# One side-work list for a whole sliding layer, stepped layer norm, and quads loaded across the chunk border, in a four-layer attention kernel

## The chip, the cores and the metric

The kernel runs on one core of a Trainium2 chip. The metric is the device time of one execution in microseconds (us). Before the change the median of three runs is 2695.69 us (2692.45 to 2696.52).

The engines are named as the profile names them: PE is the tensor engine (PEld its weight loads), DVE the vector engine, ACT the scalar engine, POOL the general engine, SP the engine that issues all the kernel's DMAs, in order (SPq is its queue).

## The reference

Four attention layers follow one another on one sequence of 2048 rows of 512: sliding, full, sliding, full. The two kinds have their own weights, each used twice. All have 32 heads of 16.

```python
def layer(x, wqkv, wo, sliding):
    h = (x - mean(x)) / sqrt(var(x) + 1e-5)              # layer norm without weights
    q, k, v = (h @ wqkv).reshape(S, 3, 32, 16)           # per head
    s = q @ k.T * 16 ** -0.5
    if sliding:                                          # 0 <= i - j < 256
        s = where(mask, s, -1e9)
    return x + (softmax(s) @ v).reshape(S, 512) @ wo

x = layer(layer(layer(layer(x, A, sliding), B, full), A, sliding), B, full)
```

## The kernel before

The sequence is cut into four **chunks** of 512 queries, and the heads into eight **quads** of four. A sliding layer runs `for c in chunks: for qd in quads: three steps`. One **step** (`attn_win`, L826) computes scores for two pairs of heads on PE (`exps`, L755, the matmuls of L768), takes the exponential on ACT (L772), lets POOL clear the edges of the window (L840, L843), and two steps later multiplies by V on PE (L850). After a quad, `epilogue` (L718) normalises the result on DVE.

Everything else is **side work** that fills PE between the steps: projections K and Q (`project`, L491), V (`values`, L640), and the output product with the residual sum (`wo`, L677). Its operands are split into two half-precision parts, so one projection is 48 groups of four matmuls (L406, 128 x 32 by 512 columns each). `mms` gives them out in pieces of four groups, 16 matmuls. K and Q go through memory: they are written there by SP (L539 to L543) and read again by quad in the order attention wants them (`load_win`, L794: three transfers, q, k and the k of the window's older half). After a K or Q, its squares are summed on PE (L559), and DVE reduces them to bounds (L575, L593, L601); that closing part waits in a list, `pend`, and `settle` (L606) issues it. `wo` is followed by layer norm of the same rows for the next layer: statistics (L439), scales, then four **parts** (`norm`, L442: L455 twice, L461) on DVE, and then four transposing DMAs on SP (`transposed`, L479, work `T`). Layer 0's own norms are the works `NN`.

The order of PE's instructions is written out by a planner when the kernel is built. It keeps a model clock (`clock`, advanced by `spent`), and each piece of side work is a generator (`Work`, L858) with a planned cost, dependencies, and the time at which it is ready. `K`, `Q`, `V` and the output product have a weight tile of 1 MB each, in a ring of two buffers; `may_open` (L884) says when a work may start loading it. A work that is `aside` is advanced by one item at each step, whatever the budget. `Side` (L919) holds the list: at each `step` it spends pieces until `cost * k / (steps - 2)` is reached, taking the first work in the list that is ready. `finish` (L1005) runs whatever is left, without attention between. The other engines' order is made by the framework's scheduler from the program order, priorities and its own model of times.

Before the change, each chunk of a sliding layer has a `Side` of its own with a list of its own (`side0(c)`, `side2(c)`, L1191 and L1200), finished when the chunk ends; only then are the first two quads of the next chunk loaded (L1042 to L1044). Within a chunk, quads are loaded two ahead, into rings of three.

Of the kernel before, what the change touches and what calls it, by code (L numbers as in the profile page):

```python
# [19 lines left out]
P = 128  # L20
NT = S // P
NC = D // P
HT = P // DH
NHT = H // HT
# [166 lines left out]
def fast_path(ctx, tc, flag, a_x, a_wqkv, a_wo, b_wqkv, b_wo, out):  # L191
# [250 lines left out]
    def norm(l, c, xs, tail=False):  # L442

        mv, y, nb, out = ST[l, c][1], [], [], []

        def scales():
            y.append(rsqrt(nc, vp, f"{l}_{c}", mv[:, :, 1]))
            if tail:
                nb.append(vp.tile([P, 4], F32, name=f"nb{l}_{c}", tag="lnb", bufs=1))
                nc.vector.scalar_tensor_tensor(nb[0], mv[:, :, 0], -1.0, y[0], op0=ALU.mult, op1=ALU.mult)  # L450

        def parts(i):
            xn = vp.tile([P, D], F32, name=f"xn{l}_{c}_{i}", tag="xn", bufs=1)
# [7 lines left out]
            nc.vector.tensor_tensor(xh[:, 1], xn, xh[:, 0], ALU.subtract)  # L461
            if tail:
                transposed(l, c, i, xh)
            else:
                out.append(xh)
        yield from turns(2, (2.4, scales), *[(1.8, lambda i=i: parts(i)) for i in range(4)])
        XN[l, c] = out
        XNR[l, c] = clock[0] + (0 if (l, c) == (0, 1) else 2 if PH["full"] else 9)
# [97 lines left out]
    def keys(l, c, act, ht=None, then=None, ring=0):  # L566
        sqs = yield from project(l, 1, c, act, ht, ring)

        def rest():
            ph = squares(f"k{l}_{c}_{ht}", sqs)  # L570
            if l not in KM:
                KM[l] = vp.tile([P, NQ], F32, name=f"km{l}", tag="km", bufs=2)
            r = quarters(ht)
            with tc.high_priority(HEAD_START):
                nc.vector.tensor_reduce(KM[l][r, c:c + 1], ph[r], axis=AX.XY if PH["full"] else AX.X, op=ALU.max)  # L575
                if then is not None:
                    then(l, ht)
        pend.append((clock[0] + (4.6 if PH["full"] else 3.6 if PH["win"] else 1.2), rest))

    def queries(l, c, act, ht=None, ring=0):  # L580
        sqs = yield from project(l, 0, c, act, ht, ring)

        def rest():
# [20 lines left out]
        pend.append((clock[0] + (4.6 if PH["full"] else 3.6 if PH["win"] else 1.2), rest))  # L604

    def settle(all_=True):  # L606
        while pend and (all_ or pend[0][0] <= clock[0]):
# [250 lines left out]
    class Work:  # L858
# [24 lines left out]

        def may_open(self):  # L884

            return (all(d in DONE for d in self.deps if d[0] == "P") and
                    all(d[1:] in ONR or d[1] % 2 == 0 and d[2] for d in self.deps if d[0] == "O") and
                    all(("N",) + d[1:] in DONE for d in self.deps if d[0] == "T") and
                    (len(wused[self.ring]) < RINGS[self.ring] or wused[self.ring][-RINGS[self.ring]].done or wused[self.ring][-RINGS[self.ring]].freed) and not (PH["win"] and self.ring)
                    and not (self.adds and any(x.adds and not x.done for x in wused[0])))  # L890
# [6 lines left out]
        def advance(self):  # L897
# [127 lines left out]
    def attention(l, works):  # L1025
# [91 lines left out]
    def OO(l, c, tail=False):  # L1117
        return Work(later(wo, l, c, tail), PO, ("N", l + 1, c), [("O", l, c, NHT - 1), ("P", l % 2, 3)], True)

    def NN(c, after=()):  # L1120
        def gen():
# [69 lines left out]
    def side0(c):  # L1191
        if c == 0:
            return [F((kw[1], True), (qs[0, 1], False), (kw[2], True), (qs[0, 2], False)), K(0, 1), Q(0, 1), PR(0, 3, [("K", 0, 1)]), VV(0, 1), PR(1, 1, [("V", 0, 1, (0, 1), 0)]), NN(2, [("T", 0, 1)]), T(0, 2)]
        if c == 1:
            return [F((kw[3], True), (qs[0, 3], False)), K(0, 2), NN(3), T(0, 3), OO(0, 0), Q(0, 2), PR(1, 0, [("P", 0, 3)]), VV(0, 2), PR(1, 2, [("P", 1, 1)]), T(1, 0), PR(1, 3, [("P", 1, 0)])]
        if c == 2:
            return [F(*[(kf, True, k, k + 1) for k in range(NQ)]), K(0, 3), OO(0, 1), Q(0, 3), VV(0, 3), K(1, 0), T(1, 1)]
        return [F(*[(qs[1, k], False) for k in range(NQ)]), K(1, 1), OO(0, 2), VV(1, 0, True, (0,)), T(1, 2), K(1, 2), Q(1, 0)]
# [26 lines left out]
    def side3(t, c):  # L1225
# [8 lines left out]
        if (t, c) != (0, 0):  # L1234
            a.append(O3(c - 1, t) if c else O3(3, t - 1))
        return a

    works = [[side0(c) for c in range(NQ)], [[last_lower(1), K1(2), upper(1, 2), upper(1, 3), K1(3)], side1()], [side2(c) for c in range(NQ)],
             [side3(t, c) for t in range(NHT) for c in range(NQ)]]
    late = lambda l: [("N", l, 3)]  # L1240
    tails = {0: [VV(1, 2, True, (0,)), OO(0, 3, True), VV(1, 1, True, (0, 1), late(1)), VV(1, 0, True, (1,), late(1)), T(1, 3), K1(0, True), K1(1, True)],
# [55 lines left out]
```

## Time and profile before

| what | us |
|---|---|
| median of three runs | 2695.69 |
| the profiled execution's own time | 2692.26 |
| its span, first to last instruction | 2690.2 |
| PE busy in the span | 2474.9 |
| ACT busy | 2363.6 |
| DVE busy | 1107.5 |
| POOL busy | 531.8 |
| first sliding layer, first to last exponential | 50.2 to 405.1 |
| second sliding layer, first to last exponential | 1406.7 to 1462.9 for its first chunk, to 1662.6 for its last |

The mean granted PE clock is 0.991 over the span. How to read the rows shown below: a row of the 40 slices gives the busy share in tenths of 1/40 of the span each. A row of busy time by stretches begins with the stretch, from and to in us, and its length; then come the busy us of PE, PEld, DVE, ACT and POOL with instruction counts in brackets (of PE alone where only PE was asked for), the granted PE clock as a share of full speed, the busy share of the DMA engines and GB/s. A row of waits names engine, operation and line, after the arrow what it waited for, then the total in us, how often, and the longest. A row of a timeline gives start, length, engine, line, operation, written and read tiles, shape and count; instructions of a kind that follow one another are merged.

### The profile page before, as it was taken

What the parts mean: (1) busy time and instruction counts of PE and PEld (TensorE: products, weight loads), DVE (VectorE), ACT (ScalarE), POOL (GpSimd) and SP (SyncE); (2) the same over time, 40 slices, a digit from 0 to 9 for tenths busy, and PEclk for the clock granted to TensorE, in tenths of its full rate; (3) what the DMA queues carried; (4) which work ended last, traced back from release to release, by engine and by line L of the source; (5) the groups of instructions that cost most, each with busy time, mean ns of one, the idle gap of its engine ahead of it and who ended that gap; (6) DMA issues with size and microseconds to landing.
All of it is one profiled execution on the core that took longest, in us unless ns stands there. A gap on an engine that the chain in (4) does not pass through costs nothing.

```text
span 2690.2 us, 120844 instructions
## 1 busy us (share of the span) xinstructions
PE 2474.9 (92%) x54767; PEld 1133.5 (42%) x54767; DVE 1107.5 (41%) x2350; ACT 2363.6 (88%) x2671; POOL 531.8 (20%) x1072
## 2 busy tenths in 40 slices
PE   7889999999998999999999999899999999999997
PEld 3344444444443444444444444544444443433332
DVE  5576453223334434434236666232333323333333
ACT  4666764999999999999996776699999999999997
POOL 1556550000000100100116886010000000000000
PEclk9999999999999999999999999999999999999999
DMA  8889875232334325324227666433333323334332
GB/s 281 254 274 268 236 198 155 69 97 86 110 94 120 97 91 148 103 87 115 92 77 211 189 171 166 128 95 105 98 97 97 106 77 114 106 98 126 126 118 93
DMA packets 341189, 361.29 MB, mean 134 GB/s; under 512 B 117800, under 2 KB 256568, under 8 KB 334392
## 3 DMA queue, kind: packets, MB, share of 16 engines
q1 hardware_dynamic: 340664, 353.46, 44.2%
q8 instruction: 430, 7.05, 1.1%
q14 instruction: 95, 0.78, 0.1%
HBM read 240.65 MB, written 96.99 MB: 126 GB/s over the span
## 4 chain that ended last, share of the span: by engine, by line
ACT 55%; PE 23%; issue 11%; DVE 6%; DMA 3%; SPq 1%; POOL 0%; ACTq 0%; DVEq 0%; POOLq 0%
ACT e L772 55%; PE b L406 7%; PE acc L850 4%; PE acc L817 3%; PE s L764 2%; PE s L768 2%; PE bs L409 2%; PE b L409 2%; PE b L402 1%; DMA kt<-kw 1%; DVE xh L461 1%; DVE xn L455 0%; DMA qs<-sp 0%; SPq L483 0%; DVE xh L455 0%
## 5 line engine op out<-in xcount | busy, mean ns | idle before, releaser
L772 ACT ACTIVATE e<-s 128x1024 f32<-128x1024 f32 (+2 forms) x2432 | 2241.6, 1056 | 143.2 <-PE s L768 104.5
L817 PE MATMUL acc<-e,vt 64*17 64x512 f32 x16384 | 1094.6, 590 | 1.9 <-issue 1.9
L764 PE MATMUL s<-qt,kt 64*32 64x512 f16 x16384 | 860.0, 381 | 123.9 <-ACT e L772 97.1
L764 PEld LDWEIGHTS <-kt 64*32 64x32 f16 x16384 | 408.2, 89 | 935.1 <-issue 853.8
L817 PEld LDWEIGHTS acc<-e,vt 64*17 64x17 f32 x16384 | 283.8, 92 | 67.9 <-issue 8.1
L843 POOL TENSOR_SCALAR_AFFINE_SELECT e<-e 128x256 f32<-128x256 f32 x512 | 230.5, 457 | 154.8 <-ACT e L772 154.1
L840 POOL TENSOR_SCALAR_AFFINE_SELECT e<-e 128x256 f32<-128x256 f32 x448 | 201.5, 456 | 96.5 <-ACT e L772 93.2
L850 PE MATMUL acc<-e,vt 128*17 128x384 f32 (+2 forms) x2816 | 202.6, 390 | 2.5 <-POOL e L840 2.2
L749 POOL TENSOR_TENSOR oh<-o,oh 128x512 f16<-128x512 f32 x31 | 36.1, 1165 | 725.1 <-DVE oh L748 725.1
L428 DVE TENSOR_SCALAR sa<-acc 128x512 f32<-128x512 f32 x64 | 44.3, 691 | 291.3 <-PE acc L817 291.3
L406 PE MATMUL b<-xc,w 128*32 128x512 f16 x2496 | 152.4, 389 | 10.8 <-DVE km L575 6.9
L714 DVE SCALAR_TENSOR_TENSOR x<-b,x 128x512 f32<-128x512 f32 x122 | 84.0, 689 | 175.1 <-PE b L402 168.4
L534 POOL TENSOR_TENSOR sq_h<-sp_h 128x512 bf16<-128x512 f16 x29 | 43.0, 1483 | 562.4 <-DVE sp_h L528 562.4
L768 PE MATMUL s<-qt,kt 64*128 64x384 f16 (+2 forms) x1408 | 120.8, 276 | 28.2 <-ACT e L772 22.7
L534 POOL TENSOR_TENSOR sq<-sp 128x512 bf16<-128x512 f16 x32 | 45.8, 1434 | 496.8 <-DVE sp L528 473.6
L402 PE MATMUL b<-xc,w 64*32 64x512 f16 x3072 | 126.4, 376 | 1.5 <-DVE j L429 0.8
L428 DVE TENSOR_SCALAR vt<-b 128x256 f32<-128x256 f32 (+1 forms) x36 | 18.4, 512 | 233.8 <-PE b L402 219.9
L402 PE MATMUL b<-wo,oh 64*32 64x512 f16 x2592 | 109.1, 376 | 4.1 <-DVE m_None L591 1.8
L402 PE MATMUL b<-xc,w_h 64*32 64x512 f16 x2784 | 111.8, 376 | 0.1
L428 DVE TENSOR_SCALAR j_h<-b 128x512 f32<-128x512 f32 x29 | 20.1, 692 | 214.6 <-PE b L402 214.6
L406 PEld LDWEIGHTS <-w 128*32 128x32 f16 x2496 | 73.5, 99 | 79.2 <-issue 27.7
L768 PEld LDWEIGHTS <-kt 64*128 64x128 f16 x1408 | 52.2, 94 | 125.7 <-issue 105.3
(142 smaller groups left out, 1942.3 us busy)
## 6 DMA issues: line engine op xcount, KB each, us to landing
kt<-kf SPq DMA_DIRECT2D x128, 512.0 KB
qt<-qs SPq DMA_DIRECT2D x128, 256.0 KB
xd<-x SPq DMA_DIRECT2D x96, 256.0 KB
x<-xd SPq DMA_DIRECT2D x96, 256.0 KB
w<-wd SPq DMA_DIRECT2D x21, 1024.0 KB
kt<-kw SPq DMA_DIRECT2D x64, 256.0 KB
qs<-sp SPq DMA_DIRECT2D x48, 256.0 KB
wo<-wd SPq DMA_DIRECT2D x12, 1024.0 KB
```

The source lines that it names most:

```text
L402: nc.tensor.matmul(ps[g:g + 32, r], a[k, g:g + 32], b[k], start=(i == 0), stop=(i == len(pairs) - 1), skip_group_check=True)
L406: nc.tensor.matmul(ps[g:g + 32], a[:, g:g + 32], b, start=(i == 0), stop=(i == len(pairs) - 1), skip_group_check=True)
L409: nc.tensor.matmul(ps, a, b, start=(i == 0), stop=(i == len(pairs) - 1))
L534: nc.gpsimd.tensor_tensor(sq, sp[:, 0], sp[:, 0], ALU.mult)
L714: nc.vector.scalar_tensor_tensor(xs[i], p, 1 / WS, xs[i], op0=ALU.mult, op1=ALU.add)
L764: nc.tensor.matmul(ps[g:g + 32, h], kt[R * h:R * h + R, pr, kc + g:kc + g + 32], qt[R * h:R * h + R, pr], start=True, stop=True, skip_grou ...
L768: nc.tensor.matmul(ps[:, h, s0:s0 + wd_], kt[R * h:R * h + R, pr, kc:kc + P], qt[R * h:R * h + R, pr, qc:qc + wd_], start=True, stop=True)
L772: nc.scalar.activation(e[:, :, w0:w1], ps[:, :, w0:w1], AF.Exp, scale=SCALE)
L817: nc.tensor.matmul(acc[r][32 * h:32 * h + DH + 1, :], V[l, qd // 4, j // 8][k, j % 8, 4 * (qd % 4) + h, :], es_[h // 2][k, h % 2, :], star ...
L840: nc.gpsimd.affine_select(v, v, pattern=[[0, 2], [-1, P]], compare_op=ALU.is_gt, fill=0.0, base=0, channel_multiplier=1)
L843: nc.gpsimd.affine_select(v, v, pattern=[[0, 2], [1, P]], compare_op=ALU.is_ge, fill=0.0, base=0, channel_multiplier=-1)
L850: nc.tensor.matmul(a[32 * h:32 * h + DH + 1, q * P:(q + nb) * P], V[l, (4 * c + j) // 4][:, j % 4, 4 * qd + h, :], es_[h // 2][:, h % 2, s ...
```

## The change

There are four edits, for the sliding layers (0 and 2) only.

1. **One list.** `attention` makes one `Side` for all 96 steps of a sliding layer. Its works are listed for the layer; `finish` runs after the last chunk. In place of the finish at each chunk's end, a chunk begins when its own K, Q and first V are done (`needs`, `lacks`) and nothing of it is in `pend` (`owes`); else side work is forced until they are. Works that only move data or prepare weights are held until their chunk begins by a dependency on `("A", l, c, 0)`, which is set when a quad starts. Output products stand earlier in the lists, and may load their weights and rows from the sixth quad of the chunk on which they depend (for the product of layer 1's last chunk, from that layer's last quad).
2. **Next chunk's first quads.** During the last two quads of a chunk, the first two of the next are loaded, if that chunk lacks and owes nothing.
3. **Layer norm in steps.** In a sliding layer `norm` yields after the scales (2.6 us of model clock) and after each part (2.4), issues the transposes itself, each two parts behind, and leaves nothing to the work `T`. Before, the parts were 2.5 us apart and `T` began 9 us after the last, one transpose every 2.3 us.
4. **At every unit.** Once an output product has given its weight buffer back (`freed`), it becomes `aside`, so that its norm advances at every step.

```diff
         yield from turns(...)   # in norm(), ahead of this line:
+        if PH["win"] and not tail:
+            scales()
+            yield wait(2.6)
+            for i in range(4):
+                parts(i)
+                yield wait(2.4)
+                if i > 1:
+                    transposed(l, c, i - 2, out[i - 2])
+            yield wait(2.0)
+            transposed(l, c, 2, out[2])
+            yield wait(2.4)
+            transposed(l, c, 3, out[3])
+            XN[l, c], XNR[l, c] = (), clock[0]
+            return
...
-            return (all(d in DONE for d in self.deps if d[0] == "P") and
-                    all(d[1:] in ONR or d[1] % 2 == 0 and d[2] for d in self.deps if d[0] == "O") and
+            return (all(d in DONE for d in self.deps if d[0] in "PA") and
+                    all(d[1:] in ONR or (d[1] % 2 == 0 and ("A", d[1], d[2], NQD - 3) in DONE or ("A", 1, d[2], NQD - 1) in DONE and d[1:3] == (1, 3)) for d in self.deps if d[0] == "O") and
...
-                self.freed = self.freed or c[0] == "freed"
+                if c[0] == "freed":
+                    self.freed = self.aside = True
...
-        sd = None
+        sd, early = None, deque()
+        if win:
+            for c in range(1, NQ):
+                for w in works[c]:
+                    if w.aside and (w.name is None or w.name[0] == "P"):
+                        w.deps = [*w.deps, ("A", l, c, 0)]
+            sd = Side(3 * NQD * NQ, [w for c in range(NQ) for w in works[c]], works[NQ])
+        needs = lambda c: [("K", l, c), ("Q", l, c), ("V", l, c, (0, 1), 0)] if l or c else []
+        lacks = lambda c: any(n not in DONE for n in needs(c))
+        owes = lambda c: any(e[2] == (l, c) for e in pend)
...
                 else:
-                    sd = Side((3 if win else NT) * len(qds), works[t * NQ + c], works[t * NQ + c + 1], 0.34 if l == 3 and t < 2 else 0.0)
-                ahead = deque([PRE.pop("w", None) or load(l, c, qds[0])])
-                if win:
+                    while lacks(c):
+                        sd.one(True)
+                    if owes(c):
+                        settle()
+                ahead, early = early, deque()
+                if not ahead:
+                    ahead.append(PRE.pop("w", None) or load(l, c, qds[0]))
+                if win and len(ahead) == 1:
                     ahead.append(load(l, c, 1))
...
                     ops = ahead.popleft()
+                    DONE["A", l, c, qd] = clock[0]
                     if qd + 1 + win in qds:
                         ahead.append(load(l, c, qd + 1 + win))
+                    elif win and c + 1 < NQ and len(early) == qd - NQD + 2 and not lacks(c + 1) and not owes(c + 1):
+                        early.append(load(l, c + 1, len(early)))
...
-                if l != 1 or c == NQ - 1:
+                if l == 3 or c == NQ - 1:
                     sd.finish(l == 3 and (t, c) != (NHT - 1, NQ - 1))
...
         if c == 1:
-            return [..., K(0, 2), NN(3), T(0, 3), OO(0, 0), Q(0, 2), ...]
+            return [..., K(0, 2), NN(3, [("T", 0, 2)]), T(0, 3), OO(0, 0, after=[("T", 0, 3)]), Q(0, 2), ...]
         if c == 2:
-            return [F(...), K(0, 3), OO(0, 1), Q(0, 3), VV(0, 3), K(1, 0), T(1, 1)]
-        return [F(...), K(1, 1), OO(0, 2), VV(1, 0, True, (0,)), T(1, 2), K(1, 2), Q(1, 0)]
-    def side2(c):
-        if c == 0:
-            return [OO(1, 3), Q(2, 2), T(2, 3), K(2, 3)]
-        if c == 1:
-            return [OO(2, 0), Q(2, 3), T(3, 0), K3(0, 0, True)]
-        if c == 2:
-            return [OO(2, 1), VV(2, 3), T(3, 1), K3(1, 0, True)]
-        return [OO(2, 2), T(3, 2), Q3(0, 0, True), K3(2, 0, True)]
+            return [F(...), OO(0, 1), K(0, 3), Q(0, 3), VV(0, 3, after=[("A", 0, 2, 1)]), K(1, 0), T(1, 1)]
+        return [F(...), OO(0, 2), K(1, 1), VV(1, 0, True, (0,)), T(1, 2), K(1, 2), Q(1, 0)]
+    def side2():
+        return [OO(1, 3), OO(2, 0), OO(2, 1), OO(2, 2), Q(2, 2), T(2, 3), K(2, 3), Q(2, 3), VV(2, 3, after=[("A", 2, 2, 1)]),
+                T(3, 0), K3(0, 0, True), T(3, 1), K3(1, 0, True), T(3, 2), Q3(0, 0, True), K3(2, 0, True)]
```

In these lists `K(l, c)`, `Q`, `VV` and `OO` are the projections and the output product of layer `l` and chunk `c`, `K3` and `Q3` a quarter of one, `T` the transposes, `NN` layer 0's norm, `PR` weight preparation and `F` constant rows in memory.

More of the change, by code (lines that the diff above doesn't have):

```diff
@@ L577, in rest @@
                     then(l, ht)
-        pend.append((clock[0] + (4.6 if PH["full"] else 3.6 if PH["win"] else 1.2), rest))
+        pend.append((clock[0] + (4.6 if PH["full"] else 3.6 if PH["win"] else 1.2), rest, (l, c)))
     def queries(l, c, act, ht=None, ring=0):
@@ L603, in rest @@
                 nc.sync.dma_start(rows(qs[l % 2, c])[8 * t:8 * t + 8, 3, :], m[32 * t:32 * t + 8, :])
-        pend.append((clock[0] + (4.6 if PH["full"] else 3.6 if PH["win"] else 1.2), rest))
+        pend.append((clock[0] + (4.6 if PH["full"] else 3.6 if PH["win"] else 1.2), rest, (l, c)))
     def settle(all_=True):
@@ L1039, in attention @@
                     settle()
-                else:
-                    sd = Side((3 if win else NT) * len(qds), works[t * NQ + c], works[t * NQ + c + 1], 0.34 if l == 3 and t < 2 else 0.0)
-                ahead = deque([PRE.pop("w", None) or load(l, c, qds[0])])
-                if win:
+                elif l == 3:
+                    sd = Side(NT * len(qds), works[t * NQ + c], works[t * NQ + c + 1], 0.34 if t < 2 else 0.0)
+                else:
+                    while lacks(c):
[6 more added lines that the diff above has]
+                if win and len(ahead) == 1:
                     ahead.append(load(l, c, 1))
@@ L1115, in VV, with OO @@
                     [("T", l, c), ("P", l % 2, 2), *after], True)
-    def OO(l, c, tail=False):
-        return Work(later(wo, l, c, tail), PO, ("N", l + 1, c), [("O", l, c, NHT - 1), ("P", l % 2, 3)], True)
+    def OO(l, c, tail=False, after=()):
+        return Work(later(wo, l, c, tail), PO, ("N", l + 1, c), [("O", l, c, NHT - 1), ("P", l % 2, 3), *after], True)
     def NN(c, after=()):
@@ L1194, in side0 @@
         if c == 1:
-            return [F((kw[3], True), (qs[0, 3], False)), K(0, 2), NN(3), T(0, 3), OO(0, 0), Q(0, 2), PR(1, 0, [("P", 0, 3)]), VV(0, 2), PR(1, 2, [("P", 1, 1)]), T(1, 0), PR(1, 3, [("P", 1, 0)])]
+            return [F((kw[3], True), (qs[0, 3], False)), K(0, 2), NN(3, [("T", 0, 2)]), T(0, 3), OO(0, 0, after=[("T", 0, 3)]), Q(0, 2), PR(1, 0, [("P", 0, 3)]), VV(0, 2), PR(1, 2, [("P", 1, 1)]), T(1, 0), PR(1, 3, [("P", 1, 0)])]
         if c == 2:
-            return [F(*[(kf, True, k, k + 1) for k in range(NQ)]), K(0, 3), OO(0, 1), Q(0, 3), VV(0, 3), K(1, 0), T(1, 1)]
-        return [F(*[(qs[1, k], False) for k in range(NQ)]), K(1, 1), OO(0, 2), VV(1, 0, True, (0,)), T(1, 2), K(1, 2), Q(1, 0)]
-    def side2(c):
-        if c == 0:
-            return [OO(1, 3), Q(2, 2), T(2, 3), K(2, 3)]
-        if c == 1:
-            return [OO(2, 0), Q(2, 3), T(3, 0), K3(0, 0, True)]
-        if c == 2:
-            return [OO(2, 1), VV(2, 3), T(3, 1), K3(1, 0, True)]
-        return [OO(2, 2), T(3, 2), Q3(0, 0, True), K3(2, 0, True)]
+            return [F(*[(kf, True, k, k + 1) for k in range(NQ)]), OO(0, 1), K(0, 3), Q(0, 3), VV(0, 3, after=[("A", 0, 2, 1)]), K(1, 0), T(1, 1)]
+        return [F(*[(qs[1, k], False) for k in range(NQ)]), OO(0, 2), K(1, 1), VV(1, 0, True, (0,)), T(1, 2), K(1, 2), Q(1, 0)]
+    def side2():
+        return [OO(1, 3), OO(2, 0), OO(2, 1), OO(2, 2), Q(2, 2), T(2, 3), K(2, 3), Q(2, 3), VV(2, 3, after=[("A", 2, 2, 1)]),
+                T(3, 0), K3(0, 0, True), T(3, 1), K3(1, 0, True), T(3, 2), Q3(0, 0, True), K3(2, 0, True)]
     def upper(l, c, tiles=range(4)):
@@ L1236, in side3 @@
         return a
-    works = [[side0(c) for c in range(NQ)], [[last_lower(1), K1(2), upper(1, 2), upper(1, 3), K1(3)], side1()], [side2(c) for c in range(NQ)],
+    works = [[side0(c) for c in range(NQ)], [[last_lower(1), K1(2), upper(1, 2), upper(1, 3), K1(3)], side1()], [side2()] + [[]] * 3,
              [side3(t, c) for t in range(NHT) for c in range(NQ)]]
```

## The prediction

> **What bounds the kernel now.** I read the page first, then busy time by stretches cut at the chunk starts of the two sliding layers, then PE's waits there, then the timelines of the waits that mattered.
>
> ```profile
> span 2690.2 us, 120844 instructions
> ...
> PE   7889999999998999999999999899999999999997
> ...
> ACT  4666764999999999999996776699999999999997
> ```
>
> The slices show where the change can act. In the full layers (slices 8 to 21 and 27 to 39 of the 40) ACT stands at 9. Around the sliding layers (slices 1 to 7 and 22 to 26) ACT falls to 4 to 7 and PE alone is near 9. So a sliding layer ends when PE has done its matmuls, and what can be won there is time that PE loses.
>
> The next rows are the eight sliding chunks, each from its first exponential to the next chunk's first (the last of a layer to its own end).
>
> ```profile
> 50.19:129.48 79.29, 66.93 (x948) 27.23 (x947) 44.47 (x107) 48.31 (x73) 42.37 (x96) 0.91 0.91 252
> 129.48:223.97 94.49, 83.07 (x1342) 38.59 (x1341) 67.06 (x155) 65.06 (x84) 55.22 (x126) 0.95 0.95 277
> 223.97:316.61 92.64, 89.94 (x1552) 43.89 (x1551) 46.66 (x114) 62.11 (x77) 52.12 (x133) 1.00 0.91 266
> 316.61:405.09 88.48, 85.53 (x1560) 43.73 (x1556) 46.74 (x111) 61.13 (x76) 51.60 (x129) 1.00 0.67 193
> 1406.74:1472.75 66.01, 62.14 (x950) 26.86 (x952) 44.40 (x105) 44.33 (x64) 41.85 (x98) 1.00 0.69 207
> 1472.75:1538.90 66.15, 62.36 (x1010) 29.33 (x1008) 45.40 (x105) 51.54 (x59) 53.12 (x128) 1.00 0.64 182
> 1538.90:1603.61 64.71, 61.80 (x1015) 28.45 (x1017) 40.82 (x98) 48.98 (x54) 53.46 (x128) 1.00 0.65 188
> 1603.61:1662.58 58.97, 53.71 (x810) 22.77 (x810) 41.27 (x98) 47.41 (x52) 49.90 (x119) 1.00 0.54 141
> ```
>
> A busy PE is not a full PE, so I price its work by its pace in undisturbed stretches (timeline of PE, layer 2):
>
> ```profile
> 1436.29 0.61 PE L768 MATMUL s<-qt,kt 64*128 64x384 f16 x8
> ...
> 1437.48 1.91 PE L406 MATMUL b<-xc,w 128*32 128x512 f16 x32
> ...
> 1440.20 1.05 PE L406 MATMUL b<-xc,w 128*32 128x512 f16 x16
> ...
> 1442.43 1.05 PE L406 MATMUL b<-xc,w 128*32 128x512 f16 x16
> 1443.41 0.61 PE L768 MATMUL s<-qt,kt 64*128 64x384 f16 x8
> ...
> 1461.67 10.54 PE L406 MATMUL b<-xc,w 128*32 128x512 f16 x192
> ...
> 1628.15 1.05 PE L406 MATMUL b<-wo,oh 128*32 128x512 f16 x16
> ...
> 1630.55 1.04 PE L406 MATMUL b<-wo,oh 128*32 128x512 f16 x16
> ```
>
> Side work comes in pieces of 16 matmuls. The block of 192 is 12 pieces in 10.54 us, so a piece costs 0.88. A step with one piece repeats after 2.39 us (1628.15 to 1630.55), so an attention step costs 1.51, and 24 steps 36.2. A first chunk has less attention: one of its quads took 7.12 (1436.29 to 1443.41) with four pieces, so 3.61, eight quads 28.9. By the code a projection (K, Q, V or the output product) is 12 pieces, half a V is 6 and a K3 or Q3 is 3. Layer 0's chunks hold 36, 48, 60 and 54 pieces, layer 2's 36, 27, 27 and 18. Span less pieces less attention is what PE **loses**: 18.8, 16.2, 3.7 and 4.9 in layer 0, and 5.5, 6.2, 4.8 and 7.0 in layer 2; together 43.6 and 23.5 us. That is all the change could win. PE's waits name most of it (the first five rows from 50 to 405 us, the last two from 1406 to 1663):
>
> ```profile
> PE s L768 <- ACT e L772: 11.3, 17, 1.4
> PE b L406 <- DVE km L575: 6.9, 1, 6.9
> PE b L559 <- DVE sp L522: 3.6, 1, 3.6
> PE b L406 <- DMA xc<-xh: 2.4, 1, 2.4
> PE s L768 <- DMA kt<-kw: 1.9, 1, 1.9
> ...
> PE s L768 <- ACT e L772: 11.3, 20, 1.1
> PE s L768 <- DMA kt<-kw: 2.0, 2, 1.4
> ```
>
> **The change part by part.** No arithmetic goes away: both lists hold the same works, so pieces and attention cost the same. What moves is when.
>
> *Quads loaded ahead (over the chunk border).* At each of six borders the six DMAs of two quads move past the end-of-chunk work on SP, in front of it. The wait for kt of 1.9 us in layer 0 goes, and so does what followed it:
>
> ```profile
> 128.77:132.20 3.43, 3.43 (x32) 0.51 1.14 371
> 162.28:166.40 4.12, 4.12 (x38) 0.50 1.02 387
> ```
>
> The granted clock was 0.51 for 3.43 us behind that wait (half of it lost, 1.7) and 0.50 for 4.12 us behind the wait of 6.9 for km (2.1 lost). So the border is worth **3.6** in layer 0. In layer 2 the two waits for kt give 2.0; I take **1.4**, the larger one, because the last border may keep its load late (below). The cover of these loads is the two quads before the border; if a chunk's K, Q or V isn't done by then (`lacks`), they are issued at the border as now, and the gain is 0.
>
> [...]
>
> *Layer norm at every unit.* The wait of 6.9 us is a queue on DVE: the last part (L455 to L461) of the fourth chunk's layer norm stands right in front of the reduction that frees a PSUM bank, and PE goes on at 162.28.
>
> ```profile
> 160.94 0.69 DVE L461 TENSOR_TENSOR xh<-xn,xh 128x512 f16<-128x512 f32 x1
> 161.55 0.68 DVE L575 TENSOR_REDUCE km<-b 128x1 f32<-128x512 f32 x1
> ```
>
> The change keeps this norm's 12 big operations and its spacing (2.4 us a part, 2.5 before), but lets it start once the third chunk is transposed, so a chunk earlier, not beside the second chunk's K work and weight preparation. DVE is busy 44.47 of 79.29 us in the first chunk and 67.06 of 94.49 in the second, so the norm moves to where there is more room. It is worth between 0 and 6.9 + 2.1 = 9.0; only PE's order is written by the planner, DVE's own order is the scheduler's, so the burst can reappear: I take **5.0**. The wait of 3.6 on the split (L522) comes from the third chunk's norm beside the first K, which the change leaves where it is: 0 (up to 3.6 + 1.7 if it goes too). The 2.4 for the first transposes lies ahead of everything moved: 0.
>
> By the planner's figures the transposes now follow their part by 4.8 us, where 9 were kept after the last one, and T is ready some 9 us sooner. What can be late next is on SP: 16 transposes a layer on an in-order queue.
>
> *One list.* Layer 2's work comes to about 97 us of planned matmul over 94 counted steps, so 1.04 us or some 1.2 pieces a step, where the four lists gave 36, 27, 27 and 18 pieces to 24 steps each. From 1443.41 to 1461.67 PE had ten attention steps and no piece: 18.3 us for ten times 1.2 (3.61 over three), so 6.2 lost, and then the block of 192, K(2,3), forced at the border. With T sooner K(2,3) can fill that stretch. But the output product of a chunk may open at the sixth quad, and it holds one of two weight buffers for nine steps before its input exists; K(2,3) then opens only when Q(2,2) ends and waits some three steps for its weights (1.9 lost). So 6.2 less 1.9, **4.3**. The last chunk, 7.0 lost with 18 pieces, gets about 28: **4.0** (0 to 7.0). The middle chunks: **1.0** beside the border. Against it, Q(2,3) and V(2,3) are due at step 72 with 75.5 us of work ahead of a budget of 74.7, so a rest is forced there, and its loads come late: **−2.2** (wait and half clock, by layer 0's border less the 1.4 above). Layer 2: 1.4 + 4.3 + 4.0 + 1.0 − 2.2 = 8.5.
>
> In layer 0 the pieces rise from 36 to about 45 in the first chunk. The steps without a piece in the second are part of its 11.3 us behind ACT, of which I take **3.0** (0 to 11.3). Buffers held by output products cost three steps at one or two borders, **−1.5**; more transfers in the first chunk, where the DMA share is 0.91, **−1.5** (0 to −3.6, one late quad). Layer 0: 3.6 + 5.0 + 3.0 − 1.5 − 1.5 = 8.6.
>
> A piece standing alone shows 1.05 us against 0.88 in the block. [...]
>
> **Sum:** 17.1 us off the profiled execution's 2692.3 us (span 2690.2 and 2.1 around it), 2675.2. The median of the runs is 2695.7, 3.4 above that execution, so the forecast is **2679**. Its own range is 2669 to 2688.
>
> **The rivals.**
>
> *Everything works (0.12).* DVE's bursts, ACT's waits and the borders all go: 3.6 + 9.0 + 5.3 + 6.0 in layer 0, 14 of 23.5 in layer 2, 38 us: 2658. For it: the third chunk of layer 0 loses only 3.7. Against: weight buffers stay two, and DVE's order is not written.
>
> *The waits move (0.23).* The fourth chunk's norm meets another K, and the no-piece steps turn up where weights are opened late. Only a border remains: 2692. For it: spacing of the parts is unchanged.
>
> *The loads ahead don't happen (0.07).* `lacks` or `owes` holds at the seventh quad nearly always; 3.6 and 1.4 fall out and −2.2 with them: 2682. Against: in layer 0 the next chunk's 36 pieces fit into 18 steps at two a step.
>
> *SP becomes the bound (0.13).* SP issues in order and already waits for others (layer 2):
>
> ```profile
> SPq L799 <- PE s L768: 34.6, 19, 4.3
> ```
>
> A transpose put closer behind its part waits for a late DVE, and behind it stand the K and Q loads of the quads. Each late quad costs 1.9 + 1.7 = 3.6. The forecast's 17.1 and another 5.4 are used up by seven late quads of 64; nine give 15.3 more than now: 2711. Against: only three loads of the 64 were late before, though SP waited up to 4.3 us at a time.
>
> **How the numbers follow.** 0.2% is 5.4 us, about what a measurement of this kernel can tell from no change. Forecast 0.45, 2658 at 0.12 and 2682 at 0.07 are faster: 0.64. The moved waits are within it: 0.23. SP: 0.13 slower. The range 2662 to 2698 leaves out some 0.08 below and the SP case above.
>
> **What would show it.** Right: the stretch 1406 to 1662 shrinks by some 8 us and layer 0's 50 to 405 by some 9; no block of 192 side matmuls before the last chunk's end; PE's wait for km gone; kt waits at most one a layer. Wrong: a DVE wait of over 3 us in front of a side matmul, L799 or L800 late in mid-chunk, clock 0.5 at new places, or full layers that change by more than 2 us, which nothing here moves.

## The result, and the profile after

The changed kernel takes 2715.73 us (median of four runs, 2710.49 to 2717.09); the kernel before, over the four runs it is compared by, 2694.39 (2692.45 to 2696.52). The ratio is 1.0075, with a 95% interval of 1.0058 to 1.0093: slower by some 20 us, where 15 us faster was forecast, and 18 us above the top of the range (2698). Code quoted here has the lines of the changed kernel; from the end of `norm` to `may_open` they are 14 higher than before (L772 is now L786, L522 is L536, L559 is L573, L575 is L589, L768 is L782).

First the page's head, the slices of PE and ACT after:

```profile
span 2715.0 us, 120828 instructions
...
PE   7969999999998999999998999999999999998997
...
ACT  4656664999999999999996777599999999999997
```

The span grew by 24.8 us (2690.2 before). To see where, I cut it at the first exponential of each layer, so that a layer holds all its own side work whichever chunk that stands in. Layers 0 and 2 before, then after, as busy time by stretches:

```profile
50.19:449.26 399.07, 367.37 (x5662) 177.41 (x5661) 225.73 (x536) 248.36 (x336) 202.43 (x484) 0.97 0.84 241
1406.74:1709.22 302.48, 283.20 (x4139) 136.89 (x4137) 192.63 (x456) 204.10 (x253) 202.09 (x482) 1.00 0.65 185
```

```profile
51.05:472.00 420.95, 368.95 (x5662) 177.40 (x5661) 226.33 (x535) 247.56 (x336) 198.39 (x484) 0.96 0.77 228
1432.11:1735.45 303.34, 280.18 (x4139) 137.34 (x4136) 186.86 (x456) 203.40 (x253) 200.08 (x482) 0.99 0.65 185
```

PE ran 5662 matmuls in layer 0 and 4139 in layer 2, both before and after: the same work. Layer 0 takes 21.9 us longer, nearly all of the loss, and PE is busy only 1.6 us longer in it; the rest is waiting. Layer 2 stands still (+0.9). From layer 1's first exponential to layer 2's it is +2.6, from layer 3's to its last +0.4; over all the runs below, whose full layers are alike, the first of these lies between 956.2 and 960.2, so such a difference says nothing.

The first four rows below are the four chunks of layer 0 after, the last is layer 2's second:

```profile
51.05:156.53 105.48, 82.29 (x1224) 35.13 (x1223) 60.73 (x149) 56.35 (x88) 39.62 (x96) 0.89 0.78 227
156.53:258.58 102.05, 86.05 (x1414) 40.51 (x1416) 53.10 (x120) 64.39 (x84) 54.23 (x132) 0.93 0.87 259
258.58:343.64 85.06, 81.95 (x1405) 39.48 (x1408) 44.85 (x108) 57.75 (x71) 53.73 (x128) 1.00 0.85 253
343.64:427.70 84.06, 76.08 (x1362) 38.18 (x1364) 46.91 (x108) 57.32 (x70) 49.27 (x124) 1.00 0.66 201
...
1489.52:1564.56 75.04, 68.19 (x1088) 31.31 (x1087) 43.76 (x104) 52.47 (x61) 52.89 (x131) 0.95 0.59 178
```

The first chunk now holds 1224 matmuls where 948 stood (17 pieces more) and would be 15.0 longer for that alone (17 by 0.88); it is 26.2 longer. By the prediction's account (span less pieces less attention) PE loses 30.0 and 20.2 us in the first two chunks, 18.8 and 16.2 before. The third loses 4.1 (3.7 before), and the fourth 11.0 (4.9): it has 42 pieces left where 54 stood, so part of what was pulled forward is missing at the end. What PE waited for, from 50 to 428 us (first four rows) and from 1431 to 1691 (last two):

```profile
PE b L573 <- DVE sp L536: 16.8, 2, 11.3
PE s L782 <- ACT e L786: 12.2, 15, 3.5
PE b L406 <- DMA wo<-wd: 11.1, 1, 11.1
...
PE b L406 <- DMA xc<-xh: 3.1, 1, 3.1
...
PE s L782 <- ACT e L786: 13.6, 23, 1.1
PE b L406 <- DVE km L589: 3.5, 1, 3.5
```

The waits for km of 6.9 and for kt of 1.9 have gone from layer 0, as forecast, and in their place stand two new waits of 11 us.

**The first, 139.54 to 150.88.** PE is to sum the squares of K for the third chunk (L573). It doesn't lack the squares: ACT finishes the last of them at 140.3 (L546). It lacks a place for the sum. Side work takes turns with two PSUM banks (tile `b`), and K's last split (L536, on DVE) has yet to read the bank whose turn it is. The timeline of DVE, with a row of ACT and PE's row at the end:

```profile
138.69 0.68 DVE L439 BATCH_NORM_STATS2 st<-x 128x6 f32<-128x512 f32 x1
...
139.63 0.63 ACT L546 ACTIVATE sq<-sp 128x512 bf16<-128x512 f16 x1
...
144.38 0.55 DVE L455 TENSOR_SCALAR xn<-x,mv,y 128x512 f32<-128x512 f32 x1
...
149.53 0.69 DVE L326 SCALAR_TENSOR_TENSOR w<-wr,w 128x512 f16<-128x512 f32 x1
150.13 0.69 DVE L536 SCALAR_TENSOR_TENSOR sp<-b,sp 128x512 f16<-128x512 f32 x1
...
150.88 0.62 PE L573 MATMUL b<-sq,hsum 128*32 128x512 bf16 x4 [11.34 <-DVE sp L536]
```

From the first row to the split DVE runs the fourth chunk's norm (statistics, scales, the first parts) and three weight preparations (L326). The split of 0.69 us stands behind 11 us of work for which nobody waits yet.

**The second, 177.84 to 188.90.** The output product of the first chunk waits for its weights. SP's issue of that load and PE's row, before and after:

```profile
157.88 0.47 SPq L371 DMA_DIRECT2D wo<-wd  x1
...
183.87 2.77 PE L406 MATMUL b<-wo,oh 128*32 128x512 f16 x48
```

```profile
179.05 0.86 SPq L371 DMA_DIRECT2D wo<-wd  x1
...
188.90 1.90 PE L406 MATMUL b<-wo,oh 128*32 128x512 f16 x16 [11.06 <-DMA wo<-wd]
```

The load is issued 21 us later than before, 1.2 us after PE had begun to wait. In the change the product stands `after=[("T", 0, 3)]`, and `may_open` demands of every such dependency that its norm, `("N", 0, 3)`, be done before the weights are fetched. With edit 3 that norm counts as done only when its last transpose has been issued, on SP at 170.06, and the load stands behind it in SP's order. So the norm that DVE ran in a block also holds back a load of 1 MB.

Behind both waits PE is slow for a while. Busy time by stretches, the granted clock third from the end:

```profile
139.54:150.88 11.34, 0.00 (x1) 0.01 (x2) 10.78 (x32) 1.18 (x3) 0.00 (x0) 0.69 0.07 23
143.90:154.10 10.20, 3.00 (x20) 0.81 (x21) 10.09 (x22) 2.50 (x3) 0.87 (x2) 0.50 0.17 39
181.50:191.70 10.20, 2.80 (x25) 0.90 (x25) 2.50 (x4) 2.42 (x5) 0.00 (x0) 0.50 0.93 346
1546.80:1553.60 6.80, 5.71 (x52) 2.10 (x55) 2.74 (x7) 1.94 (x2) 1.54 (x4) 0.50 1.06 277
```

In the first wait DVE is busy 10.78 of 11.34 us and the DMA share is 0.07: the whole core hangs on DVE's order. The clock then stays at 0.50 for 3.2 us beyond the first wait's end, 2.8 beyond the second's, 5.7 beyond the wait of 3.5 for km in layer 2. About half of that is lost: the 16 side matmuls from 188.90 take 1.90 us, where 16 took 1.05 at a clock of 1.00 (1440.20, before).

### The profile page after: what moved, and what is told of

It is laid out like the page before. It is cut to its first block, busy times and chain, and to the rows that moved or that the text cites. A ratio compares the mean times of both kernels' runs of the same rounds, so it can differ in the third digit from the quotient of the medians.

```text
span 2715.0 us, 120828 instructions
## 1 busy us (share of the span) xinstructions
PE 2475.0 (91%) x54767; PEld 1131.9 (42%) x54767; DVE 1102.9 (41%) x2350; ACT 2364.3 (87%) x2671; POOL 525.2 (19%) x1072
## 4 chain that ended last, share of the span: by engine, by line
ACT 55%; PE 24%; issue 12%; DVE 5%; DMA 2%; POOL 1%; SPq 1%; ACTq 0%; DVEq 0%; POOLq 0%
ACT e L786 54%; PE b L406 8%; PE acc L864 4%; PE acc L831 3%; PE s L782 2%; PE s L778 2%; PE bs L409 2%; PE b L409 2%; PE b L402 1%; DVE xh L461 1%; DVE xn L455 0%; POOL e L857 0%; DVE st L439 0%; DVE xh L455 0%; DMA wo<-wd 0%
## 5 line engine op out<-in xcount | busy, mean ns | idle before, releaser
L786 ACT ACTIVATE e<-s 128x1024 f32<-128x1024 f32 (+2 forms) x2432 | 2244.2, 1053 | 149.5 <-PE s L782 109.6
L857 POOL TENSOR_SCALAR_AFFINE_SELECT e<-e 128x256 f32<-128x256 f32 x512 | 227.4, 451 | 191.3 <-ACT e L786 190.4
L854 POOL TENSOR_SCALAR_AFFINE_SELECT e<-e 128x256 f32<-128x256 f32 x448 | 197.9, 447 | 95.7 <-ACT e L786 92.5
L782 PE MATMUL s<-qt,kt 64*128 64x384 f16 (+2 forms) x1408 | 121.8, 278 | 27.7 <-ACT e L786 25.8
L782 PEld LDWEIGHTS <-kt 64*128 64x128 f16 x1408 | 52.6, 94 | 126.1 <-issue 114.0
```

The costliest lines, as they stand in the source:

```text
L782: nc.tensor.matmul(ps[:, h, s0:s0 + wd_], kt[R * h:R * h + R, pr, kc:kc + P], qt[R * h:R * h + R, pr, qc:qc + wd_], start=True, stop=True)
L786: nc.scalar.activation(e[:, :, w0:w1], ps[:, :, w0:w1], AF.Exp, scale=SCALE)
L854: nc.gpsimd.affine_select(v, v, pattern=[[0, 2], [-1, P]], compare_op=ALU.is_gt, fill=0.0, base=0, channel_multiplier=1)
L857: nc.gpsimd.affine_select(v, v, pattern=[[0, 2], [1, P]], compare_op=ALU.is_ge, fill=0.0, base=0, channel_multiplier=-1)
```

## The experiments

No kernel leaves out or changes any computation; they differ in the order and time of issue alone. The edits of the change are numbered as above: 1 one list, 2 quads loaded across the border, 3 layer norm in steps, 4 at every unit. Each kernel was timed against the kernel before on the same chip (its medians there: 2693.68 beside the first four experiments, 2693.03 beside the next four, 2692.18 beside the last four). The columns "layer 0" and "layer 2" are, in the profiled execution, the time from the layer's first exponential to the next layer's, as above. They are of one execution each: in three kernels whose layer 0 is the same (before, and the first two with the change in layer 2 only) it takes 399.1, 400.0 and 397.2, so differences under 3 us in a column say nothing by themselves.

| kernel | median us | ratio (95%) | layer 0 | layer 2 |
|---|---|---|---|---|
| before | | 1 | 399.1 | 302.5 |
| after | 2715.73 | 1.0075 (1.0058 to 1.0093) | 421.0 | 303.3 |
| fourth norm held to chunk 2 | 2701.31 | 1.0028 (1.0018 to 1.0039) | 406.8 | 302.7 |
| product opens before the norm | 2714.48 | 1.0067 (1.0050 to 1.0085) | 425.3 | 305.7 |
| without 2 | 2728.92 | 1.0127 (1.0110 to 1.0144) | 430.8 | 303.4 |
| without 3 | 2701.37 | 1.0029 (1.0018 to 1.0041) | 407.7 | 299.8 |
| 1 and 2 only | 2696.32 | 1.0013 (1.0002 to 1.0023) | 408.2 | 296.2 |
| 3 and 4 only | 2694.54 | 1.0010 (1.0000 to 1.0020) | 397.7 | 302.0 |
| norm held, without 3 | 2705.45 | 1.0053 (1.0036 to 1.0070) | 412.4 | 300.6 |
| change in layer 2 only | 2691.79 | 0.9999 (0.9989 to 1.0008) | 400.0 | 301.1 |
| 1 and 2 in layer 2 only | 2686.88 | 0.9983 (0.9972 to 0.9994) | 397.2 | 296.7 |
| the same, 2 in layer 0 too | 2691.36 | 0.9998 (0.9989 to 1.0007) | 401.9 | 298.3 |
| weight preparation later | 2706.19 | 1.0050 (1.0035 to 1.0066) | 415.4 | 302.9 |
| 1 and 2, first chunk held | 2705.83 | 1.0051 (1.0036 to 1.0067) | 419.2 | 297.4 |

### The norm of the fourth chunk held back

The theory was that this norm, pulled into the first chunk, makes both new waits.

```diff
-K(0, 2), NN(3, [("T", 0, 2)]), T(0, 3),
+K(0, 2), NN(3, [("T", 0, 2), ("A", 0, 1, 0)]), T(0, 3),
```

> The changed kernel, but the fourth chunk's layer norm in layer 0 waits until the second chunk begins, as before the change. Theory 1 (the norm's burst on DVE, 139.5 to 150.9 us, is what costs): PE's wait of 11.3 us for the last split of K goes with the half clock behind it (3.3 us at 0.5, 1.6 lost), and as the norm still meets some split later, a wait of about 4 comes back: 9 us less than the changed kernel, about 2707. Theory 2 (the late weights of the output product cost, since it waits for that norm): the norm comes later, so the product is later still, no gain: 2713 to 2720. Theory 3 (loads ahead crowd SP and the DMA engines): no change, 2716.

The waits of PE in layer 0:

```profile
PE b L573 <- DVE sp L536: 7.8, 2, 5.5
PE b L406 <- DMA wo<-wd: 5.3, 2, 3.3
```

The wait of 11.3 shrinks to 2.3 (7.8 less 5.5), the one of 11.1 to two with 5.3 together, and layer 0 gets 14.2 shorter. So holding this one norm takes away some two thirds of layer 0's 21.9.

### The output product opens before that norm

```diff
-for d in self.deps if d[0] == "T") and
+for d in self.deps if d[0] == "T" and not self.norm) and
```

> The changed kernel, but an output product may open its weight tile before the layer norm that it must follow is done; its start still waits for that norm's transposes. Theory 2 (late weights): the wait of 11.1 us for wo goes with the half clock behind it (2.8 us at 0.5, 1.4 lost): 12 us less, about 2703. Against it stands that the product then holds one of two weight buffers for longer, and another projection comes late: then 2710 to 2720. Theory 1 (DVE burst): the 11.3 us stays, and theory 1 alone expects no more than these 12. Theory 3: no change, 2716.

No wait for the output product's weights is left, but another one came. Waits of PE, then of SP's queue:

```profile
PE s L782 <- DMA kt<-kw: 16.4, 1, 16.4
```

```profile
SPq L489 <- DVE xh L455: 20.5, 1, 20.5
```

With the product opened, SP has the loads of the rows x for its residual sum (L489) next in its order, and one of their buffers is still held by the norm that DVE is about to run. SP waits 20.5 us there, and the stores of K and the loads of the next quads stand behind. The demand in `may_open` did delay the weights, and without it the same late norm is paid for at another place: layer 0 is 425.3, no better than 421.0.

### Without loads across the border

```diff
-elif win and c + 1 < NQ and len(early) == ...
+elif False and win and c + 1 < NQ and len(early) == ...
```

> The changed kernel without loading the next chunk's quads in the last two quads of a chunk: they are loaded at the border. Theory 3 (the loads ahead crowd SP and the DMA engines): faster by 5 or more, under 2711. The prediction's reading (a border is worth 3.6 us in layer 0 where DMA is crowded and 1.4 in all of layer 2): slower by 3 to 6, 2719 to 2722. Theories 1 and 2 say nothing of it.

```profile
PE s L782 <- DMA kt<-kw: 14.4, 2, 7.7
```

Layer 0 is 9.8 us longer. These two waits of 6.7 and 7.7 stand at its first two borders, while the wait for the output product's weights falls from 11.1 to 2.4, so waits are also traded here; layer 2 doesn't change (303.4 to 303.3), and PE has no kt wait in it. So edit 2 does what it says, in layer 0, and there it is worth more than forecast because the one list has made the border worse: without the loads ahead the waits are 14.4 us where 1.9 stood before the change.

### Without the norm in steps

```diff
-if PH["win"] and not tail:
+if False and PH["win"] and not tail:
```

> The changed kernel with the layer norm as before: the parts 2.5 us apart with no transposes between them, the transposes 9 us of model time after the last part. Theory 1: DVE's order is made anew; in this order three of the four splits of K stand between pieces of the norm rather than one behind all of it, so the 11.3 us shrinks to some 6: about 2708. Rival (the stepping itself costs, by transposes on SP in front of loads): the whole loss goes, 2695. If the norm's form doesn't matter: 2716.

Layer 0 is 13.3 shorter than after, and layer 2 3.5. The scheduler now puts the splits between pieces of the norm, and the wait at this place is 2.6 (147 us). The load of the output product's weights is issued at 172.77, in front of the last two transposes, and PE waits 0.8 for it. The wait of 3.5 for km in layer 2 stays.

### Lists and loads only, and norm only

Two kernels halve the change: the first has 1 and 2 (the old norm, and output products that don't become `aside`), the second is the kernel before with 3 and 4.

```diff
-if PH["win"] and not tail:
+if False and PH["win"] and not tail:
...
-self.freed = self.aside = True
+self.freed = True
```

> The changed kernel with the layer norm as before and the output product not made aside, so only the one list and the loads across the border are left. If the stepping of the norm matters only by the order that DVE gets (theory 1), this is the kernel with the old norm over again: 2701, give or take 3. If making the product aside is worth something by itself, slower: 2704 to 2710. If the one list itself is the cost, no lower than 2701 either; if it costs nothing, near 2694.

> The kernel before with only the stepped norm and the product made aside: lists, finishes and loads as they were. Theory 1 (the cost is the fourth chunk's norm moved in front of a split on DVE, not its stepping): no change, 2694, give or take 4. Rival (transposes in steps hold up SP's queue): slower by 5 or more, 2699 and up.

With the two table rows of before and after, and "without 3", this takes the change apart. In layer 0 the list with its loads costs 9.1 (399.1 to 408.2), `aside` nothing (407.7), the steps 13.3 on top. The steps alone, on the old lists, cost nothing (397.7): in layer 0 they do harm only where the list lets the fourth norm start in the first chunk (with that norm held, the steps are in and layer 0 takes 406.8, no more than the list and loads alone). Part of the list's 9.1 can be seen in PE's waits of layer 0 with 1 and 2 only:

```profile
PE b L573 <- DVE sp L536: 8.1, 2, 5.5
PE b L406 <- DMA xc<-xh: 8.0, 2, 4.4
```

Before, these were 3.6 and 2.4; the 6.9 for km and the 1.9 for kt are gone. The rest isn't taken apart.

In layer 2 the list with its loads gains 6.3 (302.5 to 296.2), `aside` gives back 3.6 and the steps 3.5. Waits of PE in layer 2 with 1 and 2 only:

```profile
PE s L782 <- ACT e L786: 12.8, 25, 1.0
PE b L406 <- DVE oh L762: 0.8, 1, 0.8
```

No wait for km: it needs `aside`, since it stands in the kernel without 3 as well. Its cause on DVE in the changed kernel:

```profile
1546.47 0.77 DVE L461 TENSOR_TENSOR xh<-xn,xh 128x512 f16<-128x512 f32 x1
1547.16 0.68 DVE L589 TENSOR_REDUCE km<-b 128x1 f32<-128x512 f32 x1
```

The norm behind a layer-2 product, advanced at every step, ends right in front of the reduction for which PE waits: the pattern of the old wait in layer 0, at a new place.

### Both cures at once

> The changed kernel with both: the fourth chunk's norm held until the second chunk, and the norm as before. Theory 1: either takes away the same wait, so together they give little more than one alone: 2697 to 2702. Rival (two separate costs of 12.5 each): 2689.

The edits of "norm held" and "without 3" together. Alone they gave layer 0 14.2 and 13.3 us; together they give 8.6. PE waits once 6.8 us for ACT's exponential (to 193.70), and ACT is idle itself, in front of a weight preparation that stands before that exponential. Its raw weights were issued on SP at 185.08; the profile names no releaser ("issue"), so that ACT waits for them is my reading:

```profile
185.08 0.47 SPq L318 DMA_DIRECT2D wr<-in_B_wo_dram  x1
...
192.11 0.63 ACT L325 ACTIVATE w<-wr 128x512 f16<-128x512 f32 x1 [6.59 <-issue]
```

The two don't add up: here the room that the later norm leaves on DVE is used up by a wait in ACT's order.

### The change in layer 2 only, with and without 3 and 4

Layer 0 gets its old lists, finishes, loads and norm; layer 2 the whole change, or only 1 and 2. Two places of the edit:

```diff
-if win:      # one Side for the layer
+if l == 2:
...
-elif win and c + 1 < NQ and len(early) == ...
+elif l == 2 and c + 1 < NQ and len(early) == ...
```

> The change in the second sliding layer alone; the first sliding layer as before. The trace of the changed kernel has that layer lose as much as before (23 to 26 us before, 25 to 28 after): 2694, give or take 3. The prediction's terms for that layer (1.4 + 4.3 + 4.0 + 1.0 less 2.2) would give 2685.

> First sliding layer as before; the second with the one list and the loads across the border, but the norm as before and the output product not aside. By the profiles the second layer loses 21 us in this form (with the stepped norm 26 to 28, before 26): 5 less than before, 2688. Rival (the stepped norm is no cost in that layer, the difference is chance): as the run with the whole change in that layer, 2692 to 2694.

The whole change in layer 2 makes no difference (0.9999); 1 and 2 alone are faster than both kernels by interval, 0.9983 (0.9972 to 0.9994), 5.3 us by the medians. Layer 2 by stretches, from first exponential to the next layer's:

```profile
1405.50:1702.20 296.70, 278.85 (x4139) 136.94 (x4136) 186.96 (x456) 202.84 (x253) 202.83 (x482) 1.00 0.67 189
```

The same 4139 matmuls in 5.8 us less than before, both at a full clock. The grouping is steady over the runs: layer 2 takes 296.2 to 298.3 in the four kernels with 1 and 2 there, 299.8 and 300.6 with `aside` added, 301.1 to 305.7 in the six with 1, 3 and 4.

### Loads across the border on the old lists of layer 0

```diff
-elif l == 2 and c + 1 < NQ and ... and not lacks(c + 1) and not owes(c + 1):
+elif win and c + 1 < NQ and ... and ("K", l, c + 1) in DONE and ("Q", l, c + 1) in DONE and not owes(c + 1):
```

> The same, and in the first sliding layer, with its old lists, the next chunk's first quads are loaded ahead as soon as that chunk's K and Q are done (V isn't needed for a load; in the old lists it comes last). The border waits of that layer before (1.9 to 2.4 and up to 2.0 us, each with up to 1.7 of half clock behind it) go: 4 to 6 less than the run without it, 2683. If the loads only move the wait: no less than 2688.

The gain did not come: layer 0 is 401.9, 4.7 more than without. The border waits are gone, but new ones of 4.4 (a split, at 263.6) and 1.8 (ACT) stand elsewhere, and the km wait is 4.9 instead of 6.9.

### Weight preparation later, and the first chunk held as before

If DVE's burst were only too much work in one place, taking the weight preparations out of it should do (first edit), or keeping norm and side matmuls of the second list out of the first chunk (second edit, on top of 1 and 2, with the fourth norm held as in the first experiment).

```diff
-PR(1, 1, [("V", 0, 1, (0, 1), 0)])
+PR(1, 1, [("V", 0, 1, (0, 1), 0), ("A", 0, 1, 0)])
-PR(1, 2, [("P", 1, 1)])
+PR(1, 2, [("P", 1, 1), ("A", 0, 2, 0)])
```

```diff
-if w.aside and (w.name is None or w.name[0] == "P"):
+if w.aside and (w.name is None or w.name[0] == "P") or (l, c) == (0, 1) and w.w:
     w.deps = [*w.deps, ("A", l, c, 0)]
```

> The whole change, with two of layer 1's weight preparations later (the first held until the second chunk, the next two until the third). Theory 1, extended (what costs is DVE and ACT work that waits for late transfers in front of splits and exponentials in the first two chunks): four of DVE's 0.69 us leave the burst in front of the split, and the wait of 11.3 us shrinks to about 8, with some of ACT's wait for raw weights: 2708 to 2712. If the preparations have no part in it: 2714 to 2716. If the wait for the output product's weights goes as well: 2700.

> One list and loads across the border alone (norm as before, product not aside), but all matmul work of the second chunk's list and the fourth chunk's norm are held until the second chunk begins. If pulling that work into the first chunk is what costs in the first layer, that chunk loses 17 to 19 us as before, and not 26: about 2688. If the order inside DVE and SP is a matter of chance, anything from 2688 to 2705, with new waits at other places.

The first shortens layer 0 by 5.6, less than holding the norm: the wait of 11.3 becomes one of 2.5 and one of 4.1 (for km), that of 11.1 becomes 5.3, and new ones of 3.6 and 2.9 stand later. The second restores the first chunk (80.8 us, 79.3 before) and loses it again behind it. Its second chunk takes 118.8 where 94.5 stood, but for 69 pieces in place of 48; by the account above the four chunks lose 20.3, 22.1, 13.1 and 8.0, against 18.8, 16.2, 3.7 and 4.9 before. Waits of PE in layer 0 there:

```profile
PE b L573 <- DVE sp L536: 11.9, 2, 6.4
PE s L782 <- ACT e L786: 11.9, 19, 2.0
PE b L406 <- DMA wv<-wd: 7.1, 1, 7.1
PE b L406 <- ACT vt L684: 5.6, 1, 5.6
```

Four different producers for the same loss. That the first chunk's fill is what costs falls with it.

## Why the prediction was wrong, point by point

**The step that failed** is "the norm moves to where there is more room", worth 5.0 of a possible 0 to 9.0. The old km wait did go. But the room was counted in busy time over a whole chunk (44.47 of 79.29 us), and what counts is what stands directly in front of the operation PE needs. The norm became a block in front of the last split of K, on which a PSUM bank hung, for 11.3 us. Layer 0 was to gain 8.6 and lost 21.9; holding this norm back wins 14.2 of that again, and the list with its loads alone, the norm as before, costs 9.1. The prediction said that "the burst can reappear" and priced that as the gain not coming; a wait larger than the old one was not in its bounds, nor its range.

**A dependency I passed over.** `after=[("T", 0, 3)]` was in the diff, and the `may_open` test for norms in the kernel. Read together they tie the output product's weights to the moved norm: 11.1 us, and a clock of 0.50 for the 2.8 us behind it. I had charged the buffers held by output products with −1.5; the price was for one opened too late, not too early.

**The border** (3.6 and 1.4). Right that the kt waits go; wrong as a sum against the old trace. Of the 3.6, 1.7 was the half clock behind the wait, which doesn't follow such a wait each time (behind the same border's wait of 2.3, with 1 and 2 in layer 2 only, the clock was 1.00; last section). In layer 0 the list itself would have raised them to 14.4, and the loads ahead only undo that; on the old lists they brought nothing. Layer 2's 1.4 doesn't show (303.4 without, 303.3 with).

**Layer 0's other terms** (ACT waits 3.0, −1.5, −1.5). Behind ACT PE waits 12.2 in place of 11.3: no gain. The list with its loads alone, without the steps, loses 9.1 in this layer, so the sign of layer 0 was wrong even with the norm left out. I shifted 9 pieces forward and took the DMA share of 0.91 as its only limit; 17 came, with their splits, stores and weight preparations.

**Layer 2** (8.5). List and loads give 6.3, near it, and the block of 192 is gone: the longest run of side matmuls in layer 2 is now 48. But the sum is near by luck, not by its terms. The last chunk had 15 pieces before, not 18 (48 matmuls ran after its last exponential, at 1663.78), so it lost 9.6 and not 7.0. With 1 and 2 in layer 2 only, the four chunks lose 6.4, 5.6, 2.5 and 6.7, against 5.5, 6.2, 4.8 and 9.6: the first chunk's 4.3 isn't there, the 2.2 for a late load isn't either, and the gain lies in the third and fourth. What I priced at nothing took it back: `aside` 3.6, by the km wait of 3.5, and the steps 3.5, for which no one wait stands. I had looked for DVE's burst only in layer 0.

**The rivals.** "SP becomes the bound" gave 2711 and is the nearest in time, but not by its mechanism: no quad comes late in mid-chunk in the changed kernel. SP stuck behind a late DVE did occur, in the run that opened the product early (20.5 us). "The waits move" named the right mechanism, and priced it at no more than what had been there before.

**The list of signs.** Shown right: the block of 192, the km wait of layer 0 and the kt waits go. Shown wrong, as listed: a DVE wait of over 3 us in front of a side matmul (11.3), and half the clock at new places (0.50 from 143.90 to 154.10 and from 181.50 to 191.70). The full layers' bound of 2 us was too sharp: one execution of them scatters by 4.

**The clock behind a wait.** The prediction took the row at the border (1.9 us of waiting, followed by 3.43 us at a clock of 0.51) as what a border costs. That a wait of 1.9 can be followed by half the clock is right; that it is so each time is not, and the last section has what the runs add.

**What stays open.** In layer 0 no order was found that beats the old lists by more than noise, and most of the 9.1 that the list with its loads costs there isn't tied to single waits. Single waits can be tied to their causes, as above, but a cure's worth depends on all the others, and the order of DVE, ACT and SP that the scheduler makes can't be read off the lists.

## What to carry to other kernels

Before work is moved on an engine that is half idle, look for the next operation on that engine that the bounding engine needs, and ask how long an in-order block may stand in front of it; a mean busy share doesn't tell. Trace each moved work to every load and buffer whose opening test names it. And a wait that is taken away can be traded for another (with the output product opened early its 11.1 went, and a kt wait of 16.4 came), so try each edit alone and in each stage: here two of four edits, in one of two layers, were the whole gain.

## What the runs showed of the hardware

**Half the clock came in stretches of 3.41 us and its multiples.** In the trace before, the stretches of half clock in the layers start at 53.73, 84.45, 128.82, 159.54, 449.68 and 1712.61, and in the trace after at 58.60, 82.49, 143.93, 181.48, 208.79, 475.03, 1546.81 and 1737.96. Each is 3.41, 6.83 or 10.24 us long, and within a trace they start a whole number of 3.41 us apart. PE's busy time in the 3.41 us ahead of two of them and in their first 3.41 us, the clock third from the end; the first is the border before, the second the km wait of layer 2 after:

```profile
125.41:128.82 3.41, 1.55 (x18) 1.00 1.10 355
128.82:132.24 3.42, 3.42 (x32) 0.50 1.12 367
...
1543.40:1546.81 3.41, 1.03 (x20) 1.00 1.01 248
1546.81:1550.23 3.42, 2.34 (x22) 0.50 0.98 335
```

The border's wait of 1.86 before lay within the first of these rows, and half the clock followed though PE had been busy for 1.55 of the 3.41 us. With 1 and 2 in layer 2 only, the clock stayed full behind the same border's wait of 2.3; so it did behind the km wait of 3.5 in the run with the whole change in layer 2 only:

```profile
127.00:140.00 13.00, 12.14 (x212) 6.01 (x216) 6.25 (x14) 9.47 (x13) 7.41 (x19) 1.00 1.06 361
...
1522.11:1530.00 7.89, 7.76 (x124) 3.51 (x124) 5.37 (x12) 5.90 (x8) 4.52 (x11) 1.00 1.05 275
```

So a wait of about 2 us was followed by 3.43 us at 0.51, some 1.7 more, in one run, and by nothing of the kind in another. That it matters where the wait falls on the 3.41 us is my reading; no row here shows what decides.

**A load's latency at a DMA share of 1.06.** From SP's issue at 179.05 to PE's start at 188.90, the 1 MB weight tile took 9.9 us with the DMA share at 1.06 over the wait:

```profile
177.84:188.90 11.06, 0.00 (x0) 0.00 (x1) 3.64 (x6) 4.41 (x7) 2.21 (x6) 0.66 1.06 398
```

In the 20 us ahead of it single issues on SP took up to 4.42 us (a transposing DMA at 162.86), where others took 0.33.
